# Widening float64 weights: the last integer add on GpSimd or VectorE, held tiles, and two idle products ahead of t

## The chip, the cores and the metric

The kernel runs on one core of a Trainium2 chip. The metric is the device time of one execution in microseconds (us); shorter is better. Five engines run side by side, each through its own queue in program order: TensorE (PE, matrix products), VectorE (DVE), ScalarE (ACT), GpSimd (POOL) and SyncE (SP, which here only issues DMAs).

## The reference

The kernel computes sink and window attention for 4 batches, 8 heads, 768 positions and a head size of 64, and then a mixer and a feed-forward block on the result x (768 x 512 per batch). The feed-forward weights, U and V are float64.

```python
keep = is_sink | in_window            # 4 sinks, a window of 128
a = softmax(where(keep, q @ k.T / 8, -1e9))
x = (a @ v) as [batch, seq, 512]
xt = x.transpose(0, 2, 1)
h = xt @ U @ V                        # U: 768x32, V: 32x768
u = x + h.transpose(0, 2, 1)
ch = maximum(u @ w_ch1, 0) @ w_ch2    # 512x2048, 2048x512
return u + ch
```

## The kernel before

**Stages.** Batch 0 is done first: its attention in two halves of the sequence, then the mixer, then its feed-forward block in the plain form (`ffn`, lines 1013 to 1061), with the attention of batch 1 laid between. Batches 1 to 3 go through `ffn_joint`, which forms the product from seven smaller ones (line 1179 is its matmul); the attention of the next batches lies between these too. Products are float32 in three parts: a tile is split into a high and a low part (`uh`/`ul`, `hh`/`hl`, the two layers of `w`), so each tile of weights has to be rounded and subtracted before use.

**Weights.** The weights arrive as float64, in 32 tiles of 128x512, through four raw buffers (`big`, 512 KB a load, line 611). `narrow` (line 613) turns each into float32 with the six steps of `join_steps` (line 121): ACT or DVE takes the top half words (`nr`, lines 131, 132), ACT scales the middle words (line 133), DVE clamps (line 134) and DVE or ACT rescales (lines 135, 136) the exponent, DVE writes exponent and sign into the upper half words of `nt` (line 137), and POOL adds `nt` to the scaled middle words as 32-bit integers (line 138). The result lies in `spare` (called `flat` in the code) and is then rounded into `w` (ACT, line 596), and the rest is subtracted into `w` (DVE or POOL, lines 603, 605). U and the two halves of V go the same way first; the first four loads are issued before everything else. The first two weight blocks (numbers 8 and 9 of the order) take tiles 4 to 7: two of the first layer, in `big_94` and `big_88`, and two of the second, in `big_90` and `big_92`. The pair `w_167` holds the first layer, `w_168` the second.

**The mixer of batch 0.** `mix_half` (line 912 transposes x, line 921 multiplies with U) gathers U'x in one PSUM bank, `tp`. `mix_end` copies it to `t` (ACT, line 596), subtracts the high part on 32 partitions (DVE, line 963), and PE then multiplies `t` with V for eight pieces (line 976, each with a product of line 975 that does not need `t`); DVE adds each to x (line 978), ACT rounds (`uh`), DVE or POOL subtracts (`ul`), and the first products of the feed-forward block follow (lines 1013 to 1015, then 1035).

**Order.** Nothing is ordered by hand. `Plan` takes every step with its possible engines, its estimated time, its priority and what it needs, lays them out with a list scheduler (`forward`), gets new priorities from a pass backwards, and keeps the best of 41 rounds. `after` names steps whose planned start must come first; it adds no semaphore. A DMA is planned to land 1.5 us (`LAND`) behind its transfer. The program is the steps in the order of their planned starts, so each engine's queue is fixed; a step that waits on the chip holds back everything behind it on its engine.

Of the kernel before, what the change touches and what calls it, by code (L numbers as in the profile page):

```python
# [14 lines left out]
U16 = mybir.dt.uint16  # L15
# [6 lines left out]
P = 128  # L22
# [11 lines left out]
CH = 384  # L34
# [59 lines left out]
def words(ap):  # L94
    return ap.bitcast(I32)
# [25 lines left out]
def join_steps(nc, raw, n, a, t, out):  # L121

    x = lambda: words(raw())[:, 1:2 * n + 1:2]
    mid = lambda: raw().bitcast(U32)[:, 1:2 * n + 1:2]
# [12 lines left out]
        {"DVE": lambda: v.scalar_tensor_tensor(high(), top(), 0x8000, a(), ALU.bitwise_and, ALU.bitwise_or)},  # L137
        {"POOL": lambda: nc.gpsimd.tensor_tensor(out() if out else x(), words(t())[:, :n], x(), ALU.add)},  # L138
    ]
# [126 lines left out]
class Step:  # L266
    __slots__ = ("eng", "dur", "lat", "fn", "prio", "deps", "users", "left", "ready", "start", "n", "takes",
                 "gives", "lead", "after", "followers", "ways", "heirs", "back", "ready_b", "tiled")


class Plan:
# [7 lines left out]
    def add(self, eng, dur, fn, *args, port=False, **kw):  # L279
        return self.any({eng: (dur, fn, port)}, *args, **kw)  # L280

    def any(self, ways, r=(), w=(), prio=0.0, lat=0.0, after=(), tiled=False):
# [5 lines left out]
        s.n, s.takes, s.gives, s.tiled = len(self.steps), [], [], tiled  # L288
        s.after, s.followers = set(after), []
        deps = set()  # L290
# [37 lines left out]
    def strained(self):  # L328
# [11 lines left out]
        for _ in self.steps:  # L340
# [18 lines left out]
            if e == "SP":  # L359
                dma = max(dma, free[e] + 0.65) + s.lat  # L360
                end = dma + LAND
            for whole, users in ((True, s.users), (True, s.heirs), (False, s.followers)):
# [43 lines left out]
    def forward(self):  # L406
# [41 lines left out]
        while done < len(self.steps):  # L448
# [33 lines left out]
            if e == "SP":  # L482
                dma = max(dma, t + s.dur + 0.65) + s.lat
                end = dma + LAND
            for b in s.takes:
# [30 lines left out]
def dve(n):  # L516
    return 0.069 + n * 1.042e-3
# [6 lines left out]
def act(n):  # L524
    return 0.052 + n * 0.8333e-3
# [6 lines left out]
class Fast:  # L532
# [60 lines left out]
    def copy(self, n, dst, src, psum=False, **kw):  # L593

        nc = self.nc
        self.plan.any({"ACT": (act(n) + (0.0 if psum else 0.07), lambda: nc.scalar.copy(dst(), src()), False),  # L596
                       "DVE": (dve(n) if psum else dve2(n), lambda: nc.vector.tensor_copy(dst(), src()), not psum)},
                      **kw)
# [8 lines left out]

    def put(self, box, pair, nbytes, prio, r=(), part=None, rows=P):
        def fn():
            d, s = pair()  # L610
            self.nc.sync.dma_start(d, s)
        self.plan.add("SP", 0.5 if rows == P else 0.65, fn, r=r, w=((box, part),) if box else (), lat=nbytes / 330e3, prio=prio)

    def narrow(self, src, n, prio, flat=None):

        raw, A, T = self.raw(), self.nr(), self.nt()
        if len(self.early) > 0:
            self.early.pop(0)
        else:
            self.put(raw, lambda: (raw().bitcast(U16)[:, 1:4 * n + 1], src), P * n * 8, prio - 8.0)  # L620
        top, mid = (raw, "t"), (raw, "m")
        steps = join_steps(self.nc, raw, n, lambda: A()[:, :n], T, flat)
        use = (((top,), A), ((), mid), ((), A), ((), A), ((top, A), T), ((T, mid), flat) if flat else ((T,), mid))
        cost = (0.069 + n * 0.52e-3, 0.0, 0.069 + n * 0.26e-3, 0.069 + n * 0.26e-3, 0.05 + dve(n), 0.0)
        for ways, (r, w), c in zip(steps, use, cost):
            self.plan.any({e: (c if e == "DVE" else gps(n) if e == "POOL" else act(n) + 0.09, fn, e != "ACT")
                           for e, fn in ways.items()}, r=r, w=(w,), prio=prio)
        return (flat, lambda: f32(flat())) if flat else ((raw, "m"), lambda: f32(raw())[:, 1:2 * n + 1:2])
# [310 lines left out]
    def sink_mix(self, half, rep, t0):  # L939
# [7 lines left out]
        def run():  # L947
# [9 lines left out]
            r=(part, vsr), w=(tp,), prio=t0)  # L957

    def mix_end(self, b, t0):
        nc, add = self.nc, self.plan.add  # L960
        xT, tp, t = self.x[b], self.mixing[b][1], self.T[b]
        self.copy(DM, t, tp, psum=True, r=(tp,), w=(t,), prio=t0)
        add("DVE", dve(DM), lambda: nc.vector.tensor_tensor(
            t()[64:96], tp()[64:96], f32(t()[64:96]), ALU.subtract), r=(tp,), w=(t,), prio=t0)
        for c in range(NCHUNK):
            uh, ul = self.u[b, c] = (self.uh(), self.ul()) if b not in JOINT else (None, None)
            sl = slice(c * CH, (c + 1) * CH)
            for d in range(NC):
# [4 lines left out]
                def run(pu=pu, d=d, sl=sl, late=late):  # L973
                    if late:
                        nc.tensor.matmul(pu()[:, :CH], late[0]()[:, d, :], late[1]()[:, :CH], start=True, stop=False)
                    nc.tensor.matmul(pu()[:, :CH], t()[:, d * P:(d + 1) * P], self.vst()[:, sl], start=not late, stop=True)
                add("PE", mm(CH, 2 if late else 1), run, r=[t, self.vst] + late, w=(pu,), prio=t0)
                add("DVE", dve(CH), lambda pu=pu, x=x, sl=sl: nc.vector.tensor_tensor(
# [341 lines left out]
    def run(self):  # L1320
        tc, nc, ctx, ring, one, fixed = self.tc, self.nc, self.ctx, self.ring, self.one, self.fixed
        self.made = {}
        self.pairs, self.home, self.used = {}, {}, []
        self.T, self.u, self.x, self.sinks, self.mixing = {}, {}, {}, {}, {}
        self.gate, self.line, self.marks = (), (), [[] for _ in range(B)]
        self.wd = [[self.dram(f"wd{j}_{i}", [P, 2, 3, 2 * P], F32R) for i in range(NF // 2)] for j in range(2)]
# [356 lines left out]
```

## Time and profile before

| | |
|---|---|
| median of 3 runs | 686.84 us (686.76 to 688.16) |
| the profiled execution | 691.18 us, of which the span from first to last instruction is 689.5 us |
| mean granted clock of PE | 0.992 of full speed |
| busy in the span | PE 667.7, DVE 528.7, ACT 442.7, POOL 277.1 us |
| DMA | 191.94 MB, 278 GB/s in the mean |

The profiled execution is one run of its own, 4.34 us longer than the median of the others. Times in the rows are counted from the start of its span. A line as L976 is a line of the kernel before; numbers of buffers are left out in the trace (`big` for `big_92`).

### The profile page before, as it was taken

The numbers are of one execution on the slowest core, as the hardware profiler recorded it, in microseconds if no ns is written. First come the engines' busy times: TensorE is split into PE (matmuls) and PEld (weight loads), VectorE is DVE, ScalarE is ACT, GpSimd is POOL, SyncE is SP. The second block draws the span as 40 slices with busy tenths as digits, with TensorE's granted clock in tenths as the row PEclk, the third lists the DMA queues.
The fourth block names the chain that finished last, engine by engine and source line by source line (L and its number), as shares of the span: only waits on it lengthen the run. The fifth ranks groups of instructions, "written<-read, shape, count | busy, mean of one in ns | idle before, by whom it ended". The sixth has DMA issues, their size and how long they took to land.

```text
span 689.5 us, 12921 instructions
## 1 busy us (share of the span) xinstructions
PE 667.7 (97%) x3986; PEld 596.8 (87%) x3986; DVE 528.7 (77%) x1477; ACT 442.7 (64%) x1216; POOL 277.1 (40%) x322
## 2 busy tenths in 40 slices
PE   8996999999999999999999999999999999999997
PEld 6665887787788888888888889999999999999996
DVE  7996888889999978899787799664845983673483
ACT  6987788878675477876666995535436635543551
POOL 3554574658636353466335574211302311020121
PEclk9998999999999999999999999999999999999999
DMA  8649899979787899998899856699888889988883
GB/s 284 205 148 336 313 342 328 383 246 340 264 288 244 310 339 371 314 305 261 257 302 311 287 182 199 210 375 324 245 255 254 254 290 326 317 249 258 253 262 106
DMA packets 135982, 191.94 MB, mean 278 GB/s; under 512 B 10336, under 2 KB 106208, under 8 KB 135904
## 3 DMA queue, kind: packets, MB, share of 16 engines
q1 hardware_dynamic: 135616, 190.63, 83.1%
q8 instruction: 34, 0.56, 0.3%
q10 hardware_dynamic: 288, 0.39, 0.2%
q14 instruction: 44, 0.36, 0.2%
HBM read 141.70 MB, written 49.28 MB: 277 GB/s over the span
## 4 chain that ended last, share of the span: by engine, by line
PE 74%; DVE 13%; ACT 8%; DMA 3%; issue 1%; SPq 0%; POOL 0%; DVEq 0%; ACTq 0%
PE bank L1179 48%; PE bank L1035 6%; PE bank L720 4%; PE bank L805 3%; ACT p L732 2%; PE bank L1013 2%; PE bank L1015 2%; PE bank L1014 2%; DVE spare L603 2%; PE bank L770 2%; DVE w L603 1%; ACT oph L596 1%; DVE nt L137 1%; DMA big<-in_w_dram 1%; DMA first1q<-in_vs_dram 1%
## 5 line engine op out<-in xcount | busy, mean ns | idle before, releaser
L1179 PE MATMUL bank<-w,w 128*128 128x384 f32 x678 | 132.1, 338 | 0.0
L1179 PEld LDWEIGHTS bank<-w,w 128*128 128x128 f32 x678 | 118.2, 188 | 3.0 <-issue 1.0
L732 ACT ACTIVATE p<-p,mn 128x132 f32<-128x132 f32 x192 | 76.1, 400 | 13.2 <-DVE mn L729 13.0
L605 POOL TENSOR_TENSOR w<-uh,w 128x384 fp32r<-128x384 f32 x22 | 23.0, 1045 | 113.3 <-ACT w L596 89.1
L138 POOL TENSOR_TENSOR spare<-nt,big 128x512 int32<-128x512 int32 x32 | 46.5, 1454 | 47.0 <-DVE nt L137 20.5
L1179 PE MATMUL bank<-w,spare 128*128 128x384 f32 x342 | 65.0, 335 | 0.0
L1184 DVE TENSOR_TENSOR big<-bank,big 128x384 f32<-128x384 f32 x84 | 44.9, 553 | 23.2 <-PE bank L1179 22.9
L1035 PE MATMUL bank<-w,hh 128*128 128x512 f32 x192 | 62.2, 405 | 0.0
L1179 PEld LDWEIGHTS bank<-w,spare 128*128 128x128 f32 x342 | 59.9, 188 | 0.0
L729 DVE CUSTOM_DVE_ANT_0 p<-bank,mask 128x132 f32<-128x132 f32 x192 | 50.1, 287 | 2.6 <-PE bank L720 2.4
L720 PE MATMUL bank<-kp,qp 64*128 64x260 f32 (+1 forms) x360 | 50.1, 389 | 0.6 <-ACT oph L596 0.3
L605 POOL TENSOR_TENSOR spare<-spare 128x128 f32<-128x128 f32 (+1 forms) x54 | 35.5, 671 | 34.2 <-DMA ws<-spare 13.3
L727 DVE COPY_PREDICATED bank<-past,bank 128x128 f32<-128x128 int32 x160 | 41.7, 290 | 7.0 <-PE bank L720 6.8
L780 POOL TENSOR_SCALAR_AFFINE_SELECT oph<-oph 128x384 f32<-128x384 f32 x64 | 35.3, 566 | 28.0 <-ACT oph L596 24.9
L605 POOL TENSOR_TENSOR uh<-uh 128x384 f32<-128x384 f32 x20 | 20.5, 1025 | 62.1 <-DVE w L603 35.4
L1013 PE MATMUL bank<-ul,w 128*128 128x384 f32 x128 | 44.5, 347 | 0.0
L596 ACT CAST w<-uh 128x384 fp32r<-128x384 f32 x57 | 29.2, 514 | 22.0 <-PE bank L1179 21.0
L1015 PE MATMUL bank<-uh,w 128*128 128x384 f32 x128 | 43.2, 338 | 0.0
L1014 PE MATMUL bank<-uh,w 128*128 128x384 f32 x128 | 43.2, 338 | 0.0
L1179 PE MATMUL bank<-spare,w 128*128 128x384 f32 x204 | 43.0, 346 | 0.0
L720 PEld LDWEIGHTS bank<-kp,qp 64*128 64x128 f32 x360 | 30.4, 186 | 14.2 <-issue 5.3
L805 PE MATMUL bank<-oph,vp 128*64 128x256 f32 (+1 forms) x448 | 42.4, 338 | 0.0
(262 smaller groups left out, 1725.6 us busy)
## 6 DMA issues: line engine op xcount, KB each, us to landing
w<-ws SPq DMA_DIRECT2D x132, 256.0 KB, 4.4
w<-wd SPq DMA_DIRECT2D x102, 256.0 KB, 4.5
big<-in_w_dram SPq DMA_DIRECT2D x32, 512.0 KB, 5.9
ws<-spare SPq DMA_DIRECT2D x32, 512.0 KB, 5.3
spare<-ws SPq DMA_DIRECT2D x60, 256.0 KB, 4.3
wd<-w SPq DMA_DIRECT2D x32, 384.0 KB, 6.1
spare<-wd SPq DMA_DIRECT2D x42, 256.0 KB, 4.1
kp<-in_k_dram SPq DMA_DIRECT2D x12, 396.0 KB, 5.9
```

The lines of the kernel that those rows point to most:

```text
L138: {"POOL": lambda: nc.gpsimd.tensor_tensor(out() if out else x(), words(t())[:, :n], x(), ALU.add)},
L605: ways["POOL"] = (gps(n), lambda: nc.gpsimd.tensor_tensor(dst(), a(), b(), op), True)
L720: nc.tensor.matmul(st()[:, :wd], qr()[at, q0:q0 + P], kr()[at, k0:k0 + wd], start=True, stop=True)
L729: add("DVE", dve(SW), lambda st=st, row=row, at=at, wd=wd, qb=qb, mn=mn: nc.vector.tensor_tensor_reduce(row(), st()[:, wd - SW:wd], self.m ...
L732: add("ACT", act(SW) + 0.22, lambda row=row, at=at, mn=mn, sm=sm: nc.scalar.activation(row(), row(), AF.Exp, bias=at(mn), scale=-1.0, accu ...
L805: nc.tensor.matmul(pa()[i * D:(i + 1) * D, at:at + hi - lo], vr()[:, i, kb, :], mv, start=first, stop=last, skip_group_check=True)
L1013: nc.tensor.matmul(ph()[:, :CH], wh, ul()[:, c, :], start=n == 0, stop=False)
L1014: nc.tensor.matmul(ph()[:, :CH], wl, uh()[:, c, :], start=False, stop=False)
L1015: nc.tensor.matmul(ph()[:, :CH], wh, uh()[:, c, :], start=False, stop=n == NC - 1)
L1035: nc.tensor.matmul(acc[k](), a()[:, sl], w()[:, :, at, m:m + P].rearrange("p d o j -> p o d j"), start=not begin and i == 0 and j == 0, st ...
L1179: nc.tensor.matmul(bank()[:, :CH], w()[:, at:at + P], u()[:, d, :] if n > 1 else u(), start=first and i == 1, stop=last and i == 3 * n, sk ...
L1184: add("DVE", dve(CH), lambda: nc.vector.tensor_tensor(x(), bank()[:, :CH], t(), ALU.add), r=(bank,) if t is x else (bank, t), w=(x,), prio ...
```

## The change

1. The last step of `join_steps` has two ways. POOL adds 32-bit words as before; or DVE adds 16-bit words, the upper halves of `nt` to the upper halves of the scaled middle words, in place. The middle words of a weight tile are now scaled straight into `spare` and not back into `big`, so `big` is free once ACT has read the middle and DVE the top words.
2. Raw loads are planned to land 2.0 us (`SLOW`) later.
3. From the seventh float64 tile on (the second tile of `w_168`), the steps are planned not to start before the copy of batch 0's `t`.
4. `warm` adds a PE step of two products (mask by identity, 396 columns) between the last write to `tp` and the products of line 976; nothing reads their result.

```diff
+NWARM = 2
+NHELD = 6
+SLOW = 2.0
 def join_steps(nc, raw, n, a, t, out):
-    x = lambda: words(raw())[:, 1:2 * n + 1:2]
+    x = out or (lambda: words(raw())[:, 1:2 * n + 1:2])
+    x16 = (lambda: out().bitcast(U16)[:, 1:2 * n:2]) if out else (lambda: raw().bitcast(U16)[:, 3:4 * n + 3:4])
...
-        {"POOL": lambda: nc.gpsimd.tensor_tensor(out() if out else x(), words(t())[:, :n], x(), ALU.add)},
+        {"DVE": lambda: v.tensor_tensor(x16(), high(), x16(), ALU.add),
+         "POOL": lambda: nc.gpsimd.tensor_tensor(x(), words(t())[:, :n], x(), ALU.add)},
...
-                end = dma + LAND
+                end = dma + LAND + s.slack
...
     def narrow(self, src, n, prio, flat=None):
-            self.put(raw, lambda: (raw().bitcast(U16)[:, 1:4 * n + 1], src), P * n * 8, prio - 8.0)
+            self.put(raw, lambda: (raw().bitcast(U16)[:, 1:4 * n + 1], src), P * n * 8, prio - 8.0, slack=SLOW)
+        self.raws_seen += 1
+        held = (self.held,) if self.raws_seen > NHELD else ()
...
-                           for e, fn in ways.items()}, r=r, w=(w,), prio=prio)
+                           for e, fn in ways.items()}, r=r, w=(w,), prio=prio, after=held)
...
+    def warm(self, tp, t0):
+        nc, bank, rows = self.nc, self.bank(), self.mask.rearrange("p a b -> p (a b)")
+        def run():
+            for _ in range(NWARM):
+                nc.tensor.matmul(bank()[:, :3 * SW], self.ident, rows, start=True, stop=True)
+        return self.plan.add("PE", mm(3 * SW, 4 * NWARM), run, r=(tp,), w=(bank,), prio=t0)
...
     def mix_end(self, b, t0):
-        self.copy(DM, t, tp, psum=True, r=(tp,), w=(t,), prio=t0)
+        warm = (self.warm(tp, t0),) if b == 0 and NWARM else ()
+        s = self.copy(DM, t, tp, psum=True, r=(tp,), w=(t,), prio=t0)
+        if b == 0:
+            self.held = s
```

The scheduler lays out the whole program anew, so all five queues differ from the start on. Of the 32 last adds of weight tiles POOL keeps 12 and DVE gets 20; DVE has ten rows more than before, ACT six fewer and POOL six fewer. Two places matter below. In these rows the lines are each kernel's own: lines 596, 132 and 133 of before are 601, 136 and 137 of the change, 963 and 978 are 982 and 997, and 975 and 976 are 994 and 995.

ACT before, from the last copies of the mixer of batch 0 to the copy of `t`:

```order
L596 COPY first1q<-bank_159 128x512
L596 COPY first1k<-bank_162 128x512
L596 COPY xg_805<-bank_161 128x512
L596 CAST w_167<-spare_173 128x4x128
L133 ACTIVATE big_90<-big_90 128x512
L596 CAST w_167<-spare_173 128x4x128
L132 ACTIVATE nr<-big_92 128x512
L596 CAST t_829<-bank_165 128x512
L133 ACTIVATE big_92<-big_92 128x512
L132 ACTIVATE nr<-big_94 128x512
```

ACT after, the same place:

```order
L601 COPY first1q<-bank_160 128x512
L601 COPY first1k<-bank_161 128x512
L601 COPY xg_809<-bank_165 128x512
L601 CAST w_167<-spare_173 128x4x128
L601 CAST w_168<-spare_173 128x4x128
L601 CAST t_832<-bank_162 128x512
L136 ACTIVATE nr<-big_92 128x512
L137 ACTIVATE spare_173<-big_92 128x512
L136 ACTIVATE nr<-big_94 128x512
L137 ACTIVATE spare_174<-big_94 128x512
L601 CAST uh_863<-xT_368 128x384
L601 CAST uh_869<-xT_368 128x384
```

Before, the reading of `big_92` (the seventh tile) stood ahead of the copy of `t`; now two roundings into `w_167` and `w_168` stand ahead of it, and the seventh and eighth tile (`big_92`, `big_94`) right behind it, ahead of the roundings `uh`.

DVE after, around the subtraction of `t` (line 982); line 142 is the 16-bit add:

```order
L141 SCALAR_TENSOR_TENSOR nt<-big_90,nr 128x512
L608 TENSOR_TENSOR w_167<-spare_173,w_167 128x4x128
L142 TENSOR_TENSOR spare_173<-nt,spare_173 128x512
L608 TENSOR_TENSOR w_168<-spare_173,w_168 128x4x128
L982 TENSOR_TENSOR t_832<-bank_162,t_832 32x512
L138 TENSOR_SCALAR nr<-nr 128x512
L139 TENSOR_SCALAR nr<-nr 128x512
L141 SCALAR_TENSOR_TENSOR nt<-big_92,nr 128x512
L997 TENSOR_TENSOR xT_368<-xT_368,bank_166 128x384
L997 TENSOR_TENSOR xT_368<-xT_368,bank_163 128x384
```

The third add and the subtraction for `w_168` now stand ahead of `t`; the last three steps of the seventh tile on DVE stand between `t` and the first addition to x; before, four steps of such work (lines 134, 135, 134, 137) stood there.

On PE the two idle products stand between the last product into `tp` (line 928) and the first of line 994; they go into a bank of their own, and one product that does not need `t` still stands between them and the first that does.

ACT before, at the copy of batch 2's `t` (`t_4236`), in the middle of the program; `vsh` is the rounded `vs` of batch 3, `oph` a copy of attention weights of batch 3:

```order
L596 CAST t_4236<-bank_163 128x512
L759 COPY psink<-p_2927 128x2x3x4
L596 COPY nt<-bank_165 128x384
L596 CAST vsh_4250<-first1q 128x512
L596 COPY oph_4261<-bank_160 128x3x128
L732 ACTIVATE p_2889,sm<-p_2889,mn 128x132 x3
L1227 ACTIVATE uh_3039<-bank_166 128x384
```

ACT after, the same place (`t_4123`):

```order
L601 CAST t_4123<-bank_166 128x512
L739 ACTIVATE p_2916,sm<-p_2916,mn 128x132
L601 COPY oph_4140<-bank_165 128x3x128
L601 COPY oph_4149<-bank_163 128x3x128
L739 ACTIVATE p_2916,sm<-p_2916,mn 128x132 x3
L601 COPY nt<-bank_160 128x384
L746 ACTIVATE r<-sm 128x6
L601 CAST vsh_4173<-first1q 128x512
L601 CAST spare_174<-spare_174 128x4x128 x2
```

Before, the copy into `oph_4261` stood behind the rounding of `vsh`, which needs a load; now two such copies stand ahead of it.

## Rows read from the trace of the kernel before

**Rows 1.** The page: the span, and busy time of PE.

```profile
span 689.5 us, 12921 instructions
...
PE 667.7 (97%) x3986; PEld 596.8 (87%) x3986; DVE 528.7 (77%) x1477; ACT 442.7 (64%) x1216; POOL 277.1 (40%) x322
```

**Rows 2.** Timeline of PE: start, us, instruction, and idle time before it with releaser.

```profile
54.55 0.74 PE L975 MATMUL bank<-xhl,vsh 128*128 128x384 f32 x1
61.49 0.69 PE L976 MATMUL bank<-vst,t 128*128 128x384 f32 x1 [6.19 <-DVE t L963]
...
68.04 0.34 PE L1013 MATMUL bank<-ul,w 128*128 128x384 f32 x1
```

**Rows 3.** Timeline of ACT ahead of t.

```profile
59.59 0.65 ACT L132 ACTIVATE nr<-big 128x512 bf16<-128x512 bf16 x1 [4.49 <-DMA big<-in_w_dram]
60.15 0.57 ACT L596 CAST t<-bank 128x512 fp32r<-128x512 f32 x1
```

**Rows 4.** The chain that ended last, around 52 us: start, us, what.

```profile
51.98 7.24 DMA big<-in_w_dram
```

**Rows 5.** Windows: stretch, its us, busy PE, PEld, DVE, ACT, POOL, PEclk, DMA share, GB/s.

```profile
61.50:66.90 5.40, 5.40 (x17) 5.30 (x18) 4.67 (x11) 5.09 (x11) 4.49 (x4) 0.50 1.02 390
62.00:205.00 143.00, 140.76 (x805) 116.91 (x804) 127.69 (x351) 115.07 (x310) 84.71 (x86) 0.98 0.89 316
180.00:200.00 20.00, 18.74 (x118) 15.75 (x118) 19.25 (x35) 13.03 (x25) 9.13 (x7) 1.00 0.77 263
363.80:367.20 3.40, 3.40 (x13) 3.29 (x13) 2.74 (x8) 0.36 (x2) 2.14 (x2) 0.50 0.78 302
450.00:684.00 234.00, 234.00 (x1344) 234.00 (x1343) 143.16 (x276) 112.96 (x231) 41.33 (x39) 1.00 0.86 273
```

**Rows 6.** Timeline of DVE from the end of attention to the additions to x.

```profile
44.52 1.01 DVE L776 TENSOR_TENSOR oph<-bank,tri 128x384 f32<-128x384 f32 x2
45.45 0.58 DVE L137 SCALAR_TENSOR_TENSOR nt<-big,nr 128x384 uint16<-128x384 uint16 x1
46.06 0.73 DVE L603 TENSOR_TENSOR vst<-big,vst 32x384 fp32r<-32x384 f32 x1
...
50.37 1.55 DVE L603 TENSOR_TENSOR vst<-big,vst 32x384 fp32r<-32x384 f32 x1
...
52.91 0.28 DVE L134 TENSOR_SCALAR nr<-nr 128x512 bf16<-128x512 bf16 x1
53.22 1.37 DVE L135 TENSOR_SCALAR nr<-nr 128x512 uint16<-128x512 uint16 x1
...
55.74 0.67 DVE L603 TENSOR_TENSOR w<-spare,w 128x512 fp32r<-128x512 f32 x1
60.74 0.69 DVE L963 TENSOR_TENSOR t<-bank,t 32x512 fp32r<-32x512 f32 x1 [4.33 <-ACT t L596]
...
62.98 2.41 DVE L978 TENSOR_TENSOR xT<-xT,bank 128x384 f32<-128x384 f32 x5
```

**Rows 7.** Groups by line and form: count, busy us, mean ns, idle before.

```profile
L138 POOL TENSOR_TENSOR spare<-nt,big 128x512 int32<-128x512 int32 x32 | 46.5, 1454 | 47.0 <-DVE nt L137 20.5 <-ACT w L596 7.0 <-ACT nr L132 2.8
L134 DVE TENSOR_SCALAR nr<-nr 128x512 bf16<-128x512 bf16 x32 | 16.0, 499 | 1.0 <-ACT nr L132 0.9
L135 DVE TENSOR_SCALAR nr<-nr 128x512 uint16<-128x512 uint16 x19 | 8.9, 470 | 0.2
```

**Rows 8.** Timeline of DVE and PE around 100 us: a weight tile finished, and used.

```profile
100.92 1.06 DVE L603 TENSOR_TENSOR w<-spare,w 128x512 fp32r<-128x512 f32 x1
...
102.96 0.68 DVE L603 TENSOR_TENSOR w<-spare,w 128x512 fp32r<-128x512 f32 x1
...
105.08 0.74 PE L1035 MATMUL bank<-w,hh 128*128 128x512 f32 x2
```

**Rows 9.** Timeline of ACT and PE around 361 us, the mixer of batch 2.

```profile
360.97 0.62 ACT L596 CAST vsh<-first1q 128x512 fp32r<-128x512 f32 x1 [2.01 <-DMA first1q<-in_vs_dram]
...
362.61 1.43 PE L976 MATMUL bank<-vst,t 128*128 128x384 f32 x3 [1.35 <-DVE oph L776]
```

More of the change, by code (lines that the diff above doesn't have):

```diff
@@ L267 @@
     __slots__ = ("eng", "dur", "lat", "fn", "prio", "deps", "users", "left", "ready", "start", "n", "takes",
-                 "gives", "lead", "after", "followers", "ways", "heirs", "back", "ready_b", "tiled")
+                 "gives", "lead", "after", "followers", "ways", "heirs", "back", "ready_b", "tiled", "slack")
 class Plan:
@@ L288, in any @@
         s.n, s.takes, s.gives, s.tiled = len(self.steps), [], [], tiled
-        s.after, s.followers = set(after), []
+        s.after, s.followers, s.slack = set(after), [], 0.0
         deps = set()
@@ L483, in forward @@
                 dma = max(dma, t + s.dur + 0.65) + s.lat
-                end = dma + LAND
+                end = dma + LAND + s.slack
             for b in s.takes:
@@ L595, in copy @@
         nc = self.nc
-        self.plan.any({"ACT": (act(n) + (0.0 if psum else 0.07), lambda: nc.scalar.copy(dst(), src()), False),
+        return self.plan.any({"ACT": (act(n) + (0.0 if psum else 0.07), lambda: nc.scalar.copy(dst(), src()), False),
                        "DVE": (dve(n) if psum else dve2(n), lambda: nc.vector.tensor_copy(dst(), src()), not psum)},
@@ L606, in tt, with put @@
         self.plan.any(ways, **kw)
-    def put(self, box, pair, nbytes, prio, r=(), part=None, rows=P):
+    def put(self, box, pair, nbytes, prio, r=(), part=None, rows=P, slack=0.0):
         def fn():
@@ L611, in fn @@
             self.nc.sync.dma_start(d, s)
-        self.plan.add("SP", 0.5 if rows == P else 0.65, fn, r=r, w=((box, part),) if box else (), lat=nbytes / 330e3, prio=prio)
+        self.plan.add("SP", 0.5 if rows == P else 0.65, fn, r=r, w=((box, part),) if box else (), lat=nbytes / 330e3, prio=prio).slack = slack
     def narrow(self, src, n, prio, flat=None):
@@ L619, in narrow @@
         else:
-            self.put(raw, lambda: (raw().bitcast(U16)[:, 1:4 * n + 1], src), P * n * 8, prio - 8.0)
+            self.put(raw, lambda: (raw().bitcast(U16)[:, 1:4 * n + 1], src), P * n * 8, prio - 8.0, slack=SLOW)
         top, mid = (raw, "t"), (raw, "m")
+        self.raws_seen += 1
+        held = (self.held,) if self.raws_seen > NHELD else ()
         steps = join_steps(self.nc, raw, n, lambda: A()[:, :n], T, flat)
-        use = (((top,), A), ((), mid), ((), A), ((), A), ((top, A), T), ((T, mid), flat) if flat else ((T,), mid))
-        cost = (0.069 + n * 0.52e-3, 0.0, 0.069 + n * 0.26e-3, 0.069 + n * 0.26e-3, 0.05 + dve(n), 0.0)
+        use = (((top,), A), ((mid,), flat) if flat else ((), mid), ((), A), ((), A), ((top, A), T), ((T,), flat or mid))
+        cost = (0.069 + n * 0.52e-3, 0.0, 0.069 + n * 0.26e-3, 0.069 + n * 0.26e-3, 0.05 + dve(n), dve(n))
         for ways, (r, w), c in zip(steps, use, cost):
             self.plan.any({e: (c if e == "DVE" else gps(n) if e == "POOL" else act(n) + 0.09, fn, e != "ACT")
-                           for e, fn in ways.items()}, r=r, w=(w,), prio=prio)
+                           for e, fn in ways.items()}, r=r, w=(w,), prio=prio, after=held)
         return (flat, lambda: f32(flat())) if flat else ((raw, "m"), lambda: f32(raw())[:, 1:2 * n + 1:2])
@@ L976, in run @@
                     nc.tensor.matmul(pu()[:, :CH], t()[:, d * P:(d + 1) * P], self.vst()[:, sl], start=not late, stop=True)
-                add("PE", mm(CH, 2 if late else 1), run, r=[t, self.vst] + late, w=(pu,), prio=t0)
+                add("PE", mm(CH, 2 if late else 1), run, r=[t, self.vst] + late, w=(pu,), prio=t0, after=warm)
                 add("DVE", dve(CH), lambda pu=pu, x=x, sl=sl: nc.vector.tensor_tensor(
@@ L1324, in run @@
         self.T, self.u, self.x, self.sinks, self.mixing = {}, {}, {}, {}, {}
+        self.raws_seen, self.held = 0, None
         self.gate, self.line, self.marks = (), (), [[] for _ in range(B)]
```

## The prediction

> **What bounds the kernel now.** I read the page first, for the engine that is full: PE is busy for 97% of a span of 689.5 us [rows 1]. Then the windows, to see whether that holds in every stage: from 450 to 684 us PE is busy without a break [rows 5], so whatever an earlier stage gains or loses reaches the end undiminished. Then PE's timeline, for the holes. The largest stands behind the mixer of batch 0: PE ends a product of line 975 at 55.29 and starts line 976 at 61.49, 6.19 us later, on DVE's `t` [rows 2]. ACT's timeline says why: the copy of `t` starts at 60.15, behind a reading of `big` that waited for a DMA until 59.59 [rows 3]; the chain has that load, 7.24 us from 51.98 on [rows 4]. Then the windows for the clock: it stands at 0.50, the lower of its two levels, from 61.5 to 66.9 us, right behind the hole [rows 5]. A second such place lies at 361 us: ACT waits until 360.97 for the load of `vs` for batch 3, PE waits 1.35 us on attention work that is queued behind it [rows 9], and the clock is at 0.50 again from 363.8 to 367.2 [rows 5].
>
> **The sum, first term: t.** I count from O, the end of the last two line-776 steps of batch 0's attention on DVE, 44.52 + 1.01 = 45.53 [rows 6]. Up to there both orders have nearly the same work, so I leave O in place; an error of 1 us in it goes straight into the time. Before, DVE was done with its own work at 55.74 + 0.67 = 56.41, that is O + 10.9, and `t` reached PE at O + 16.0. In the new order ACT's copy of `t` no longer stands behind a load that is still under way, but behind two roundings that need DVE's adds; so DVE's queue sets `t`. Between O and `t` DVE gets three adds and one subtraction more, and one line-137 step of 384 columns, one subtraction on V and one line-134 step fewer. For the add, which the trace doesn't have on DVE, the nearest row is a two-input step of 128x512, 0.68 us [rows 8]; the lower bound is a 16-bit step with one input, 0.28 [rows 6], the upper one the same two-input step beside POOL, 1.06 [rows 8]. I take 0.68, since the add has two inputs. That makes 4 x 0.68 - 0.58 - 0.73 - 0.28 = +1.1 us, so O + 12.0. Before, three DVE steps in this stretch were stretched while POOL added: line 135 took 1.37 and a subtraction on V 1.55, against 0.28 for line 134 and 0.73 for the other half of V [rows 6]. POOL now has two such adds there instead of four; I take off 0.8 us of these 1.9, and add 0.69 for `t` itself [rows 6]: O + 11.9, 4.1 us earlier. It can't be before O + 11.1, since `tp` ends about when PE stops, at 55.29 (O + 9.8), and copy, subtraction and start took 61.49 - 60.15 = 1.34 us [rows 2, 3]; without any relief it is O + 12.7.
>
> The idle products lie in the hole of 11.9 - 9.8 = 2.1 us, where PE would wait anyway. The trace has none of their kind there: with 396 columns each they take at least as long as a line-1013 product, 0.34 us [rows 2], and I bound them at four times that, so 0.7 to 2.7 us for both. The sum takes them as hidden; the upper bound would add 0.6 us. I take it that the clock stays up over what is left of the hole; if it does not, the price is 5.4 / 2 = 2.7 us [rows 5].
>
> **Second term: from t to the feed-forward block.** Before, its first product (line 1013) started at 68.04, 6.55 us behind the first of line 976 [rows 2], 5.4 of them at half clock [rows 5]. At full clock PE alone would need 6.55 - 2.7 = 3.9 us. But DVE has eight additions to x of 2.41 / 5 = 0.48 us each [rows 6], 3.9 us, and ahead of them three steps on the seventh tile, at 0.28, 0.28 and, scaled from 0.58 for 384 columns, 0.77 us, 1.3 us. So the block starts 5.2 us behind `t`, not 3.9, at O + 17.1; before it was O + 22.5. Together 5.4 us earlier. The load for the seventh tile must have landed by then: it is issued behind the second V half, about O + 4, not O + 6.4 (51.98), and with the 7.24 us of [rows 4] lands at O + 11.3, just ahead of `t`.
>
> **Third term: the second place.** In the new order the attention copies of batch 2 stand ahead of the copy of `vs` on ACT, and the pieces with `t` are spread between other products. What is there to win is 1.35 us of waiting and 3.4 / 2 = 1.7 of half clock [rows 5, 9], 3.05 in all. The whole order is new, so another stall can take its place: I count 1.5.
>
> **What it gives back.** Of the 20 adds on DVE 17 come after `t`. At 0.68 that is 11.6 us more on an engine that is busy for 127.7 of 143 us between 62 and 205 us [rows 5]. Against it stands relief from POOL: lines 134 and 135 took 499 and 470 ns in the mean [rows 7] where an undisturbed one takes 280 [rows 6], 32 x 0.22 + 19 x 0.19 = 10.6 us over 32 adds of POOL, so 5.6 for 17. Net 6 us: 133.7 of 143 is 93%, below the 96% that DVE reaches from 180 to 200 us (19.25 of 20) [rows 5]. So the stage need not grow, but PE waits oftener for steps that come late: I count 1.5 us. The sum is -5.4 - 1.5 + 1.5 = -5.4 us. The profiled execution took 691.18 us, 4.34 more than the median of the others; the difference is taken from the median, 686.84 - 5.4 = **681.4 us**.
>
> **Two rules weighed.** The rows price the add as any two-input step, 0.68, and the low end of 0.28 would take 17 x 0.4 = 6.8 us off DVE. The Trainium skill (VectorE: DVE Perf Modes, What auto-detection actually checks) gives 16-bit operands the faster rate only where neighbours lie next to each other; upper half words do not, so by it the add costs the full 0.68 and the half words buy no speed. No run here shows the add yet. For the stretched steps the rows show 1.37 beside a POOL add. The Trainium skill (GPSIMD Engine Reference, Key points) says that GpSimd shares its SBUF interfaces with VectorE; by it the relief should come with each add moved, and the sum stays as it is, while without relief it would lose another 5.6 us of DVE time.
>
> **The rivals.** *The weights come no earlier.* A tile finished at 102.96 + 0.68 = 103.64 was used at 105.08 [rows 8], 1.4 us later. If the loads hold the pace (DMA share 0.89 from 62 to 205 us [rows 5]), the block starts early and then waits, and of the 5.4 us 1.4 are left: 685.4, by the third term at best 684. For it: the share. Against it: `big` is free one POOL add (1.45 us [rows 7]) earlier, and the loads behind O are issued some 2 us earlier.
> *t is as late as before.* ACT's copy now waits for the roundings, these for DVE's third add, and that for a load. Should this chain be 4 us slower than walked, the change does nothing: 686.8.
> *DVE becomes the bound.* If the adds run beside POOL at 1.06 us and there is no relief, DVE gets 18 us more: 145.7 at a filling of 0.963 needs 151.3 us in place of 143, +8.3, against -5.4 at its start and nothing from the third term: 689.7. It decides above 0.963 x (143 + 5.4) - 127.7 = 15.2 us of added work, 0.9 us an add.
> *The clock falls all the same*, behind a short wait as at 361 us: +2.7, 684.1, within the forecast's range.
>
> **Chances.** Forecast 0.56, its own range 677.0 to 684.1; weights 0.16 (684 to 686); t late or the planner's gain used up elsewhere 0.13 (about 686.8); DVE the bound 0.15 (688.3 to 691). A change under 0.2%, 1.4 us, can't be told from none with this kernel. Below 685.4: 0.56 and most of 0.16, together 0.70; between 685.4 and 688.2: 0.15; above: 0.15. The range for 8 in 10 leaves out the slow rival and a tail below: 677.0 to 688.2.
>
> **What would show it.** Right: the wait of line 995 (976 before) on `t` under 2 us, no stretch at 0.50 behind it, line 1032 (1013 before) starting about 62.6 us, the 16-bit add at 0.6 to 0.8 us, lines 138 and 139 nearer 300 than 480 ns, PE busy without breaks up to 137 us. Wrong: ACT idle on a DMA ahead of `t`; DVE's three steps for the seventh tile waiting for their load; PE waits on `w` around 95 to 100 us; more than 3 us of new holes between 137 and 450 us.

## The result, and the profile after

The changed kernel takes **681.99 us** (median of 5 runs, 680.54 to 683.21) against 686.84 us before (5 runs, 686.38 to 689.47): a ratio of 0.9911, with a 95% interval of 0.9891 to 0.9932, so 0.9% faster. The profiled execution is the one of 681.99 us, with a span of 680.2 us. The forecast was 681.4, within 677.0 to 684.1. The spans of the two profiled executions differ by 9.3 us, more than the medians, since the one of before was itself 4.3 us above its median.

The page answers to [rows 1]:

```profile
PE 665.4 (98%) x3990; PEld 595.0 (87%) x3990; DVE 532.9 (78%) x1498; ACT 438.7 (64%) x1197; POOL 256.1 (38%) x310
```

DVE has 4.2 us and 21 instructions more than before, ACT 19 and POOL 12 instructions fewer. PE's timeline answers to [rows 2]. Lines 972, 994, 995 and 1032 are the idle products, lines 975, 976 and 1013 of before:

```profile
54.67 1.50 PE L972 MATMUL bank<-mask,ident 128*128 128x396 f32 x4
55.70 0.64 PE L994 MATMUL bank<-xhl,vsh 128*128 128x384 f32 x1
57.82 0.45 PE L995 MATMUL bank<-vst,t 128*128 128x384 f32 x1 [1.48 <-DVE t L982]
...
62.66 0.44 PE L1032 MATMUL bank<-ul,w 128*128 128x384 f32 x1 [0.57 <-POOL ul L610]
```

The hole on `t` is 1.48 us, not 6.19, and the block starts at 62.66, not 68.04. (The two idle products stand as four matmuls in the records.) ACT's timeline answers to [rows 3]:

```profile
55.70 0.62 ACT L601 CAST w<-spare 128x512 fp32r<-128x512 f32 x1 [1.54 <-DVE spare L142]
56.23 0.58 ACT L601 CAST t<-bank 128x512 fp32r<-128x512 f32 x1
56.70 0.66 ACT L136 ACTIVATE nr<-big 128x512 bf16<-128x512 bf16 x1
```

DVE's timeline answers to [rows 6]:

```profile
44.98 1.01 DVE L783 TENSOR_TENSOR oph<-bank,tri 128x384 f32<-128x384 f32 x2
...
54.89 0.72 DVE L142 TENSOR_TENSOR spare<-nt,spare 128x512 uint16<-128x512 uint16 x1
56.35 0.69 DVE L608 TENSOR_TENSOR w<-spare,w 128x512 fp32r<-128x512 f32 x1 [0.74 <-ACT w L601]
57.08 0.69 DVE L982 TENSOR_TENSOR t<-bank,t 32x512 fp32r<-32x512 f32 x1
```

The copy of `t` now waits for DVE's adds (line 142) and a rounding, no longer for a load; the reading of `big` behind it (line 136) finds its load landed. SP issued the loads behind the second V half at 49.93, not at 51.98 (SP's timeline):

```profile
49.93 0.80 SPq L616 DMA_DIRECT2D big<-in_w_dram  x2
```

O, the end of batch 0's attention on DVE from which the prediction counts, is 44.98 + 1.01 = 45.99. The windows answer to [rows 5] (PE, PEld, DVE, ACT, POOL busy, granted clock, DMA share, GB/s):

```profile
45.99:57.77 11.78, 10.35 (x66) 6.35 (x64) 9.38 (x19) 9.62 (x20) 1.98 (x3) 1.00 0.72 224
55.00:62.00 7.00, 5.52 (x26) 4.23 (x24) 6.10 (x12) 5.51 (x11) 2.65 (x3) 1.00 1.03 397
62.00:67.00 5.00, 4.08 (x22) 3.68 (x22) 5.00 (x12) 3.84 (x9) 1.84 (x2) 1.00 1.03 410
62.00:205.00 143.00, 142.03 (x821) 118.01 (x821) 137.30 (x377) 110.77 (x293) 76.39 (x80) 1.00 0.90 324
340.00:350.00 10.00, 10.00 (x63) 9.84 (x62) 8.89 (x29) 7.83 (x25) 8.07 (x12) 1.00 0.95 316
```

The clock is at 1.00 behind `t` and at the second place (here the copy of batch 2's `t` starts at 340.75), and DVE has gone from 127.69 to 137.30 of 143 us. The groups answer to [rows 7]:

```profile
L142 DVE TENSOR_TENSOR spare<-nt,spare 128x512 uint16<-128x512 uint16 x20 | 17.9, 894 | 0.3 <-ACT spare L137 0.2
L138 DVE TENSOR_SCALAR nr<-nr 128x512 bf16<-128x512 bf16 x32 | 12.0, 379 | 0.1
L139 DVE TENSOR_SCALAR nr<-nr 128x512 uint16<-128x512 uint16 x15 | 4.2, 282 | 0.1
L143 POOL TENSOR_TENSOR spare<-nt,spare 128x512 int32<-128x512 int32 x12 | 19.0, 1584 | 33.1 <-DVE nt L141 24.3 <-ACT spare L137 3.6 <-ACT nr L136 3.2
```

The new add takes 894 ns in the mean, 720 to 740 in the three that stand ahead of `t`. The clamp (line 138) fell from 499 to 379 ns, the rescale (line 139) from 470 to 282.

### The profile page after: what moved, and what is told of

It reads as the page before. It is cut to its first block, busy times and chain, and to the rows that moved or that the text cites. A ratio compares the mean times of both kernels' runs of the same rounds, so it can differ in the third digit from the quotient of the medians.

```text
span 680.2 us, 12939 instructions
## 1 busy us (share of the span) xinstructions
PE 665.4 (98%) x3990; PEld 595.0 (87%) x3990; DVE 532.9 (78%) x1498; ACT 438.7 (64%) x1197; POOL 256.1 (38%) x310
## 4 chain that ended last, share of the span: by engine, by line
PE 83%; DVE 10%; DMA 3%; ACT 2%; issue 1%; POOL 1%; SPq 0%; ACTq 0%; DVEq 0%
PE bank L1198 48%; PE bank L1054 10%; PE bank L727 5%; PE bank L812 4%; PE bank L1032 3%; PE bank L1033 3%; PE bank L1034 3%; PE bank L777 2%; DVE p L736 1%; PE bank L919 1%; DMA kp<-ud 1%; DMA w<-wd 1%; DVE w L608 1%; DVE bank L734 1%; DVE oph L783 1%
## 5 line engine op out<-in xcount | busy, mean ns | idle before, releaser
L610 POOL TENSOR_TENSOR w<-uh,w 128x384 fp32r<-128x384 f32 x22 | 23.2, 1054 | 105.7 <-ACT w L601 102.6
L610 POOL TENSOR_TENSOR spare<-spare 128x128 f32<-128x128 f32 (+1 forms) x56 | 39.2, 705 | 43.0 <-DVE spare L608 17.8
L727 PE MATMUL bank<-kp,qp 64*128 64x260 f32 (+1 forms) x360 | 52.9, 392 | 1.1 <-DMA qp<-in_q_dram 0.4
L734 DVE COPY_PREDICATED bank<-past,bank 128x128 f32<-128x128 int32 x160 | 41.5, 289 | 4.5 <-PE bank L727 4.3
L787 POOL TENSOR_SCALAR_AFFINE_SELECT oph<-oph 128x384 f32<-128x384 f32 x64 | 33.8, 546 | 27.3 <-ACT oph L601 27.0
L601 ACT CAST w<-uh 128x384 fp32r<-128x384 f32 x57 | 29.3, 515 | 20.1 <-PE bank L1198 17.9
L812 PEld LDWEIGHTS bank<-oph,vp 128*64 128x64 f32 x448 | 28.5, 137 | 14.9 <-issue 3.9
L608 DVE TENSOR_TENSOR spare<-spare 128x128 f32<-128x128 f32 (+1 forms) x84 | 36.5, 459 | 6.2 <-DMA ws<-spare 3.1
```

The costliest lines, as they stand in the source:

```text
L610: ways["POOL"] = (gps(n), lambda: nc.gpsimd.tensor_tensor(dst(), a(), b(), op), True)
L727: nc.tensor.matmul(st()[:, :wd], qr()[at, q0:q0 + P], kr()[at, k0:k0 + wd], start=True, stop=True)
L734: add("DVE", dve(P), lambda st=st: nc.vector.copy_predicated(st()[:, SW:UW], self.past, st()[:, :P]), w=(st,), prio=t0)
L812: nc.tensor.matmul(pa()[i * D:(i + 1) * D, at:at + hi - lo], vr()[:, i, kb, :], mv, start=first, stop=last, skip_group_check=True)
```

## The experiments

Besides the change twelve kernels ran, in three groups on three chips. Medians of different chips can't be set against each other, so each is told by its ratio to the kernel before on its own chip. "Block" is the start of the feed-forward block in the one profiled execution, "idle" the time that PE stood idle in it from there to 455 us (the window less PE's busy time).

| kernel | ratio | 95% interval | median us | block | idle |
|---|---|---|---|---|---|
| before | 1 | | 686.84 | 68.04 | 5.5 |
| the change | 0.9911 | 0.9891 to 0.9932 | 681.99 | 62.66 | 1.9 |
| tiny_idle | 0.9919 | 0.9891 to 0.9947 | 681.67 | 64.20 | 2.5 |
| add_twice | 1.0162 | 1.0136 to 1.0188 | 698.67 | 65.66 | 10.6 |
| add_cut | 0.9904 | 0.9879 to 0.9930 | 681.00 | 62.86 | 2.0 |
| pool_cut | 0.9900 | 0.9879 to 0.9922 | 681.30 | 62.36 | 1.6 |
| b_t_first | 0.9991 | 0.9974 to 1.0009 | 687.34 | 65.93 | 3.7 |
| b_hold | 0.9882 | 0.9857 to 0.9907 | 679.22 | 65.34 | 1.8 |
| b_add | 0.9894 | 0.9866 to 0.9923 | 679.86 | 63.23 | 1.8 |
| hold_add | 0.9980 | 0.9965 to 0.9995 | 686.48 | 62.58 | 6.1 |
| no_slow | 0.9910 | 0.9888 to 0.9932 | 682.21 | 63.57 | 2.2 |
| pool_adds | 0.9966 | 0.9948 to 0.9984 | 685.86 | 65.81 | 6.2 |
| b_same1 | 0.9965 | 0.9945 to 0.9985 | 686.16 | 65.83 | 4.9 |
| b_same2 | 0.9978 | 0.9965 to 0.9992 | 686.71 | 64.59 | 4.2 |

Two of these windows, of the change and of hold_add:

```profile
62.66:455.00 392.34, 390.47 (x2378) 337.33 (x2379) 345.36 (x1009) 281.45 (x801) 186.04 (x220) 1.00 0.87 301
62.58:455.00 392.42, 386.28 (x2350) 330.43 (x2351) 345.50 (x1018) 272.83 (x795) 180.45 (x209) 1.00 0.86 297
```

tiny_idle, add_twice, add_cut and pool_cut keep the change's order on every engine, b_t_first that of before, and alter one thing in it. The others leave parts of the change out or put them in alone, and the planner lays everything out anew.

### One thing altered in a fixed order

**b_t_first**: only `t`, one place earlier.

```diff
-        return sorted(self.steps, key=lambda s: (s.start, s.n))
+        seq = sorted(self.steps, key=lambda s: (s.start, s.n))
+        i = seq.index(self.first)            # the ACT copy of batch 0's t
+        j = max(k for k in range(i) if seq[k].eng == "ACT")
+        late = seq.pop(j)                    # line 132 on big_92
+        seq.insert(i, late)
+        return seq
```

> The kernel before with its own order on every engine but for one exchange on ACT: the copy of batch 0's t now stands ahead of the reading of big_92 that waited for its load. Nothing else of the change. If the prediction's first two terms are right, t comes at about 57.2 us instead of 61.5, the half-clock stretch behind it is gone, the block starts at 62 to 63, and the time falls by 4 to 6 us against the kernel before. If the weights or DVE hold the pace behind it: the block starts early, PE waits later, and 0 to 2 us are left.

ACT's timeline of this run:

```profile
55.43 0.59 ACT L602 CAST t<-bank 128x512 fp32r<-128x512 f32 x1
58.61 0.67 ACT L132 ACTIVATE nr<-big 128x512 bf16<-128x512 bf16 x1 [2.60 <-DMA big<-in_w_dram]
```

PE's, in which lines 984 and 1021 are the first product with `t` and the block's first:

```profile
57.46 0.45 PE L984 MATMUL bank<-vst,t 128*128 128x384 f32 x1 [1.90 <-DVE t L971]
...
65.93 0.44 PE L1021 MATMUL bank<-ul,w 128*128 128x384 f32 x1 [2.04 <-POOL ul L611]
```

DVE's, in which line 986 is the additions to x:

```profile
59.32 0.29 DVE L134 TENSOR_SCALAR nr<-nr 128x512 bf16<-128x512 bf16 x1 [1.91 <-ACT nr L132]
...
60.63 0.29 DVE L134 TENSOR_SCALAR nr<-nr 128x512 bf16<-128x512 bf16 x1 [0.69 <-ACT nr L132]
...
61.61 3.81 DVE L986 TENSOR_TENSOR xT<-xT,bank 128x384 f32<-128x384 f32 x8
```

`t` comes at 57.46 as expected, 4 us earlier than in [rows 2]. But on DVE steps for the seventh and eighth tile stand ahead of the additions to x, and they wait for ACT's readings behind that load (1.91 and 0.69 us), so the additions start at 61.61 and the block starts at 65.93, 3.3 us later than in the change. Of the time nothing measurable is left: 0.9991, where 4 to 6 us were expected if the first two terms are right. An earlier `t` by itself buys nothing that can be measured; the wait on the load goes over from PE's wait on `t` to DVE's queue behind it.

**tiny_idle**: the idle products nearly without work.

```diff
-                nc.tensor.matmul(bank()[:, :3 * SW], self.ident, rows, start=True, stop=True)
+                nc.tensor.matmul(bank()[:, :8], self.ident, rows[:, :8], start=True, stop=True)
```

> The changed kernel with its own order on every engine, but the two idle products cut from 396 columns to 8 each, so that PE stands idle through the hole ahead of t. If the short hole (1.5 to 2 us) alone leaves the granted clock up: 682.0 us within 0.7, and no stretch at 0.50 near 58 us. If the idle products hold the clock: a stretch at 0.50 behind line 995, up to 2.7 us more, 683.5 to 684.7.

PE's timeline of this run:

```profile
56.24 0.51 PE L972 MATMUL bank<-mask,ident 128*128 128x8 f32 x4
...
59.38 0.44 PE L995 MATMUL bank<-vst,t 128*128 128x384 f32 x1 [2.35 <-DVE t L982]
```

Its windows:

```profile
10.00:20.00 10.00, 8.82 (x40) 5.68 (x41) 9.44 (x62) 9.70 (x49) 5.50 (x9) 0.53 0.72 237
...
55.00:60.00 5.00, 2.65 (x12) 1.67 (x11) 4.11 (x9) 3.36 (x7) 0.00 (x0) 1.00 0.97 362
60.00:65.00 5.00, 4.46 (x23) 3.85 (x23) 4.96 (x10) 4.17 (x10) 4.09 (x4) 1.00 1.04 406
```

PE waited 2.35 us and the clock stayed at 1.00; the time is that of the change. In this order the work of the idle products brings nothing that can be measured. (The times here are 1.5 us later than the change's from the end of the stretch at 0.53 between 10 and 20 us on; the change's profiled execution doesn't have that stretch, with the same order.)

**add_twice, add_cut, pool_cut**: what an add costs.

```diff
-{"DVE": lambda: v.tensor_tensor(x16(), high(), x16(), ALU.add),
+{"DVE": lambda: (v.tensor_tensor(x16(), high(), x16(), ALU.add), v.tensor_tensor(high(), high(), x16(), ALU.add)),   # add_twice
+{"DVE": lambda: v.tensor_tensor(x16()[:, :8], high()[:, :8], x16()[:, :8], ALU.add),                                # add_cut
-"POOL": lambda: nc.gpsimd.tensor_tensor(x(), words(t())[:, :n], x(), ALU.add)},
+"POOL": lambda: nc.gpsimd.tensor_tensor(x()[:, :8], words(t())[:, :8], x()[:, :8], ALU.add)},                       # pool_cut
```

> The changed kernel with its own order, but behind each 16-bit add on VectorE a second one of the same shape, whose result nothing reads: about 20 x 0.72 to 0.89 = 14 to 18 us more work on DVE, 12 to 15 of it behind t. If DVE's filling decides, as the prediction's rival has it (96% between 62 and 205 us, already 137.3 of 143 busy): the stage grows by 6 to 10 us, 688 to 692. If PE's reserve of finished weights takes it up: under 2 us, 682 to 684.

> The changed kernel with its own order, the 20 adds on VectorE cut from 512 to 8 columns (the output is not the reference's). It leaves out about 20 x 0.8 = 16 us of DVE work. If DVE has the reserve that the prediction gave it (give-back 1.5 us): 679.5 to 681.5. If DVE's time in the first 250 us is PE's time, as in the doubled adds (+16.9 us for 20 of them): 665 to 669.

> The changed kernel with its own order, the 12 adds left on POOL cut from 512 to 8 columns (the output is not the reference's): 12 x 1.6 = 19 us less of POOL work. If POOL's adds stretch DVE's steps as the prediction took it (0.33 us an add) and DVE decides: 3 to 5 us faster than the change, with line 138 down from 379 to about 330 ns. If there is no relief and POOL is not waited for: 681 to 682.5.

The window from 62 to 205 us of add_twice:

```profile
62.00:205.00 143.00, 135.09 (x750) 109.61 (x749) 138.94 (x361) 102.86 (x278) 72.23 (x75) 0.98 0.85 297
```

Its groups of the two adds:

```profile
L142 DVE TENSOR_TENSOR nt<-nt,spare 128x512 uint16<-128x512 uint16 x20 | 19.2, 961 | 0.7
L142 DVE TENSOR_TENSOR spare<-nt,spare 128x512 uint16<-128x512 uint16 x20 | 17.8, 892 | 0.3 <-ACT spare L137 0.2
```

The same window of add_cut:

```profile
62.00:205.00 143.00, 142.10 (x823) 118.13 (x822) 129.01 (x378) 110.93 (x293) 73.04 (x80) 1.00 0.91 329
```

Its group of the add:

```profile
L142 DVE TENSOR_TENSOR spare<-nt,spare 128x8 uint16<-128x8 uint16 x20 | 5.5, 274 | 0.3 <-ACT spare L137 0.2
```

The same window of pool_cut:

```profile
62.00:205.00 143.00, 142.24 (x822) 118.29 (x823) 135.01 (x378) 110.29 (x293) 64.46 (x80) 1.00 0.89 325
```

Its groups of the clamp and the add (the rescale, line 139, took 302 ns):

```profile
L138 DVE TENSOR_SCALAR nr<-nr 128x512 bf16<-128x512 bf16 x32 | 10.4, 330 | 0.1
L142 DVE TENSOR_TENSOR spare<-nt,spare 128x512 uint16<-128x512 uint16 x20 | 16.8, 840 | 0.3 <-ACT spare L137 0.2
```

19.2 us more on DVE cost 1.0162 - 0.9911 = 2.5%, 17 us: nearly all of it, and more than either expectation had. 17.9 - 5.5 = 12.4 us less gave 0.0007, nothing that can be measured. So less work on DVE brings the changed kernel nothing, and much more work costs nearly its full length. If each us beyond some edge costs one, that edge lies about 2 us above the change; this is an estimate from two points, and whether the second adds cost by filling DVE or by delaying their own tiles was not told apart. In add_twice PE does only 135.09 us of work in the window in which the change does 142.03, with DVE at 97%. The adds on POOL do stretch DVE's steps (line 138 from 379 to 330 ns, the add from 894 to 840, DVE's window from 137.30 to 135.01), but of the time nothing measurable came of it.

### The parts of the change, each with a new order

**b_hold** and **b_add** are the kernel before with one part alone; **hold_add** has both; **no_slow** has both and the idle products; **pool_adds** is the change without the DVE way. Wherever the DVE way is in, and in pool_adds too, the middle words are scaled into `spare`; the cut below leaves these lines out.

```diff
+        self.raws_seen += 1                                  # b_hold, hold_add
+        held = (self.held,) if self.raws_seen > 6 else ()
-                           for e, fn in ways.items()}, r=r, w=(w,), prio=prio)
+                           for e, fn in ways.items()}, r=r, w=(w,), prio=prio, after=held)
...
+        {"DVE": lambda: v.tensor_tensor(x16(), high(), x16(), ALU.add),   # b_add, hold_add; taken out in pool_adds
...
-SLOW = 2.0                                                   # no_slow
+SLOW = 0.0
```

> The kernel before with the hold alone: from the seventh float64 tile on the steps are planned behind the copy of t; no 16-bit adds, no later landing, no idle products. By the prediction's first two terms the hold brings t to O + 12 to 13 instead of O + 16.0, and the time to 682 to 684; if the clock falls in the hole, which here has no idle products, 684 to 686. If the gain is that of the adds moved to DVE: 686.8 within 1.4.

> The kernel before with the two ways of the last add alone (about 20 of 32 adds on DVE, middle words scaled into spare); no hold, no later landing, no idle products. In its order ACT reads big twice more ahead of the copy of t. By the prediction the load is still waited for and t stays within 1.5 us of O + 16: 685 to 688. If the gain comes from the adds on DVE and from POOL's relief: 681 to 683, with lines of the clamp and the rescale near 0.3 us.

> The kernel before with the hold and the two ways of the last add (21 adds on DVE), without the later landing and the idle products. Each alone gave 679 to 680. If they cure the same hole and the adds cost nothing beyond it: 679 to 680.5. If the adds take DVE time that the hold alone didn't need (16.9 us more for doubled adds): 681 to 683, as the whole change. If their gains add: 672 to 675.

> The changed kernel with SLOW at 0 in place of 2.0: hold, both ways of the add and idle products stay, the order is laid out anew. If the later landing is what makes hold and adds go together (hold and adds without it gave a ratio of 0.998): 0.996 to 1.000 of the kernel before. If orders scatter by several us: anywhere from 0.988 to 1.000.

> The changed kernel without the DVE way: all 32 last adds on POOL, with hold, later landing and idle products. If the adds on DVE are what holds the change back behind the hold alone (682.0 against 679.2): 678 to 680. If the later landing and the idle products are: 681 to 683. If the relief of POOL carries the gain: 684 to 687.

The hold alone gives 0.9882 and the adds alone 0.9894, each as much as the whole change. Both together give 0.9980, and with the idle products added 0.9910, though tiny_idle shows their work to be worth nothing in a fixed order. pool_adds, the hold with the later landing and the idle products, gives 0.9966 where the hold alone gave 0.9882. Parts with an effect of their own don't combine in this way. Of the expectations, b_hold and b_add came out faster than any range named, hold_add slower than all three; no_slow failed the first of its two and is within the scatter of the second. In b_add nothing waited for a load ahead of `t`, against what was expected: its wait on `t` was 1.23 us. pool_adds fell where the relief of POOL was to carry the gain, but the hold alone, with all adds on POOL, speaks against that reading. PE's timeline of hold_add, in which lines 982 and 1019 are the first product with `t` and the block's first:

```profile
57.81 0.44 PE L982 MATMUL bank<-vst,t 128*128 128x384 f32 x1 [1.23 <-DVE t L969]
...
62.58 0.44 PE L1019 MATMUL bank<-ul,w 128*128 128x384 f32 x1 [0.49 <-POOL ul L607]
```

PE's timeline of b_hold, in which these are lines 980 and 1017:

```profile
59.66 0.44 PE L980 MATMUL bank<-vst,t 128*128 128x384 f32 x1 [1.84 <-DVE t L967]
...
65.34 0.34 PE L1017 MATMUL bank<-ul,w 128*128 128x384 f32 x1
```

hold_add starts the block where the change does, and is 0.7% slower; b_hold starts it 2.7 us later, and is at least as fast. Where the block starts does not settle the time.

### A new order and nothing else

**b_same1** and **b_same2**: one planner cost moved by 2 ns, the time that the planner allows between two dependent steps of one engine.

```diff
-SAME = 0.11
+SAME = 0.112      # b_same1; 0.108 in b_same2
```

> The kernel before with none of the change; one planner cost differs by 0.002 us (SAME 0.112 for 0.11), so that the whole order is laid out anew. On ACT the reading of big_92 still stands ahead of the copy of t. If the 61-us hole is what the hold and the adds cured: the wait on t stays near 6 us and the time at 686 to 689. If orders scatter by several us whatever the change does: a time anywhere from 680 to 690.

> The kernel before with none of the change and the same planner cost at 0.108. On ACT three readings of raw buffers (big_92 once, big_94 twice) stand ahead of the copy of t, more than before, so that t waits for a later load: if t's place decides, the time is 687 to 692. If orders scatter by several us whatever the change does: anywhere from 680 to 690.

Both are faster than before, by 0.35% and 0.22%, with nothing of the change in them. PE's timeline of b_same1, in which ACT still reads `big` ahead of `t`:

```profile
59.39 0.69 PE L976 MATMUL bank<-vst,t 128*128 128x384 f32 x1 [4.41 <-DVE t L963]
```

The hole of 4.41 us is there and the time is lower all the same. b_same2, with three such readings ahead of `t`, was expected at 687 or more if the place of `t` decides, and was at 686.71 against 688.22, with a wait on `t` of only 2.30 us: that expectation failed. Both lie within the scatter that the other one named.

## Why the prediction was right, and where its reasons were not

**Term 1, t: right at its place, in part by luck.** `t` at O + 11.8 (57.82 - 45.99), forecast O + 11.9; the hole 1.48 us, forecast under 2. As forecast, no load is waited for and DVE's adds set `t`. But the sum had DVE at work for nearly all of that time, 10.62 us as before + 1.1 - 0.8 + 0.7 = 11.6; it worked for 9.38 and waited for 2.4, on ACT and PE. No step was stretched there (POOL had one add, where the sum took two and took off 0.8 us), and the chain from DVE to ACT and back, 0.74 us of it behind the last add, was not in the sum. The two misses cancel.

**Term 2, the block: right at its place.** Line 1032 at O + 16.7, forecast O + 17.1, 4.84 us behind `t`, and the 5.38 us between the two profiles is the 5.4 of the sum. b_t_first shows what carries this: `t` alone brings 2.1 us of it at the block and nothing measurable in the time. Most of the rest hangs on the load of the seventh tile, which the prediction had as a side condition ("must have landed by then") and which the change issues 2 us earlier.

**The step that failed** is the one that made a gain of the kernel out of these two terms: "whatever an earlier stage gains or loses reaches the end undiminished". It was read off PE's solid stretch from 450 us on; between the block's start and that stretch PE has small holes, and these move with every new order. I added up, from the records of PE, the time from one matmul's start to the next less what is usual for its shape (the lower quartile of that shape in the kernel before, 0.173 us for 128x384), in us: up to the block's start, from there to the last product of line 1054 (1035 before), and from there to 455 us.

| | to the block | in the block | to 455 us |
|---|---|---|---|
| before | 46.9 | 33.8 | 51.2 |
| the change | 40.2 | 30.9 | 49.7 |
| hold_add | 41.5 | 33.3 | 52.4 |
| b_hold | 44.2 | 29.5 | 47.2 |

From before to the change that is 6.7 + 2.9 + 1.5 us, of which 0.5 is lost again at the end and 1.3 goes into the idle products: the 9.3 us between the spans. hold_add wins 5.4 us ahead of the block, as forecast, and has 5.1 us more than the change behind it. The forecast counted -1.5 and +1.5 for all that lies behind the block; two orders whose kernels differ in the idle products alone lie 0.7% apart, some 5 us (hold_add against no_slow), as much as the whole sum. So 681.4 came out as the right number, and the profile's first 63 us are as forecast, but that the one is the cause of the other is not shown, and how much of the agreement is luck can't be told. b_same1 and b_same2 put a quarter to two fifths of the gain (0.22% and 0.35% of 0.89%) within reach of an order drawn without any of the change.

**The clock.** The stretch at 0.50 behind `t` is gone in this profile, as forecast. The idle products neither kept it up elsewhere nor were needed for it: no_slow, with the same ones and a wait of 1.98 us, has the clock at 0.81 and 0.85 from 55 to 65 us, and tiny_idle, nearly without them, has it at 1.00 behind 2.35 us. That one apart, the clock stayed up in the profiles with waits on `t` of 1.23 to 1.53 us (hold_add, b_add, pool_adds, the change, pool_cut) and fell in those with 1.84 to 6.19 (b_hold, b_t_first, no_slow, b_same2, add_twice, b_same1, before). With one profile a kernel, how much of the 2.7 us in term 2 belongs to the order and how much to the execution stays open; the five runs of the change, in one order, have mean clocks from 0.991 to 0.999.

**Third term, the second place.** From 340 to 350 us the clock is at 1.00 and PE busy throughout, so all of the 3.05 us is gone in this profile, more than the forecast's 1.5. But b_t_first, with before's order at this place, has the clock at 1.00 there too, and PE idle for only 0.7 us:

```profile
350.00:370.00 20.00, 19.32 (x124) 16.00 (x124) 18.08 (x72) 14.34 (x54) 11.73 (x14) 1.00 0.96 330
```

So most of the loss that the forecast read at 361 us belonged to one execution, and its end can't be counted as a gain of the change.

**The give-back: right in sign, its reserve too large.** The add took 0.72 to 0.74 us ahead of `t`, near its price of 0.68, and 0.894 in the mean. That price was the mis-sized term: 17 x (0.894 - 0.68) = 3.6 us, by which DVE came to 137.30 of 143 and not to 133.7; add_cut shows that this cost nothing. The two lines fell by what was counted: (499 - 379) x 32 + (470 - 282) x 15 = 6.7 us for 20 adds, 0.33 each, as the prediction had it. That the moved adds are the cause is not shown: with all 32 on POOL the clamp took 399 ns in b_hold and 637 in b_same2 (line 134 in both), and 481 in b_add with 19 of them on DVE.

```profile
L134 DVE TENSOR_SCALAR nr<-nr 128x512 bf16<-128x512 bf16 x32 | 12.4, 399 | 0.1
L134 DVE TENSOR_SCALAR nr<-nr 128x512 bf16<-128x512 bf16 x32 | 20.1, 637 | 1.5 <-ACT nr L132 1.4
```

In a fixed order pool_cut took 49 x 32 + 54 x 20 - 20 x 15 ns, 2.3 us, off the clamp, the add and the rescale, 0.2 for each of the 12 adds that it cut. The rival "DVE becomes the bound" was put at 15.2 us of added work. In the whole span DVE has 532.9 - 528.7 = 4.2 us more than before, so 11 should be left, and add_twice, with 19.2 more, should have lost 8; counted from 62 to 205 us it is 137.30 - 127.69 = 9.6 us more, 5.6 left and at most 14 lost. It lost 17, more than either.

**The rules.** That 16-bit operands spaced apart get no faster rate (the Trainium skill, VectorE: DVE Perf Modes, What auto-detection actually checks): the trace agrees, 0.72 us and not 0.28. That GpSimd shares its interfaces with VectorE (the Trainium skill, GPSIMD Engine Reference, Key points): the trace agrees, with pool_cut's 379 to 330 ns. That the relief comes with each add moved, as the prediction took from it, is not borne out: the clamp of b_hold and b_same2 says otherwise.

**What stays open.** Why the orders fall into a group near 0.99 (the change, b_hold, b_add, no_slow) and one from 0.9965 up (before, b_t_first, hold_add, pool_adds, both b_same). I found no single wait that tells them apart, but the table's last column shows where they part: from the block's start to 455 us PE stood idle for 1.8 to 2.2 us in the first group and for 3.7 to 6.2 in the second, while ahead of the block the sums of the two overlap. That is part of the some 5 us between them; each figure is from one profile. What fills these holes in one order and not in the next is not known; b_hold in before's fixed order, and many orders of one kernel, weren't tried. The profiled execution of before, at 691.18 us, is a long one: of 63 later runs of that kernel on three other chips one was longer.

**The better version.** b_hold, 679.22 us and 0.9882, is the simplest and has the lowest ratio; its interval overlaps the change's, so a lead over the change is not shown.

## What to carry to other kernels

Where a scheduler lays the whole program out again, first measure what a meaningless nudge of its costs does; a gain not well above that is not yet the edit's. Curing a wait by moving one instruction is worth only what the other queues behind it let through: move it alone, in the old order, before counting it. And measure a reserve from both sides, by cutting the work and by doubling it: here the one gave nothing and the other cost nearly all of it.

## What the runs showed of the hardware

In these profiles the granted clock followed neither the order nor the length of a wait alone: with one order on every engine it stood at 1.00 from 10 to 20 us in one execution (the change) and at 0.53 in another (tiny_idle); behind a wait of 2.35 us it stayed up (tiny_idle), behind one of 1.90 us it fell (b_t_first, windows):

```profile
55.00:60.00 5.00, 3.10 (x12) 2.54 (x11) 2.96 (x6) 2.31 (x5) 1.58 (x1) 0.83 0.88 295
60.00:65.00 5.00, 3.57 (x13) 2.34 (x11) 4.34 (x10) 5.00 (x11) 3.82 (x4) 0.83 1.02 404
```

Part of an instruction's time does not shrink with its columns: the 16-bit add over 512 columns took 724 ns at the least and 754 in the median (the change), over 8 columns 152 and 162 (add_cut); on POOL the 32-bit add took 1289 and 1342 ns, and 192 and 250 over 8 columns (pool_cut). The means of 894 and 274 ns on DVE hold a few that took up to 1867 and 1276 ns:

```profile
L142 DVE TENSOR_TENSOR spare<-nt,spare x20: 724/754/1867, 49.9 to 193.6; 128x512 uint16<-128x512 uint16 x20
L142 DVE TENSOR_TENSOR spare<-nt,spare x20: 152/162/1276, 51.5 to 193.2; 128x8 uint16<-128x8 uint16 x20
```
